# An FFT mixer with two MLPs on Trainium2: two fetches later, five subtractions on another engine, the units at a step's head

## The chip, the cores and the metric

One core of one Trainium2 chip runs the whole program. The metric is the device time of one execution in microseconds (us); of several runs the median is given. TensorE is called PE below, VectorE DVE, ScalarE ACT, GpSimd POOL, SyncE SP; SP issues nearly all transfers, in the order of its queue.

## The reference, cut to what matters

```python
X = np.fft.rfft(x, axis=1)                       # x: 4 x 3136 x 256, float32
y = np.fft.irfft(X * (filt_r + 1j * filt_i), n=3136, axis=1)

u = y + ((y.transpose(0, 2, 1) @ U) @ V).transpose(0, 2, 1)      # U: 3136 x 32
x = u + np.maximum(u @ w_ch1, 0.0) @ w_ch2                       # 256 -> 1024 -> 256

xn = (x - mean(x)) / np.sqrt(var(x) + 1e-06) * g_ln
out = x + np.maximum(xn @ w1b, 0.0) @ w2b
```

U, V and the weights of both MLPs are float64; the kernel works on their bits and cuts them into a high and a low float32r part. Products in the first MLP are made of three matmuls (high by high, high by low, low by high).

## The kernel before, in words

The Fourier transform of length 3136 is done as products with tables, in stages of 56 and 28 points. Batch 0 is transformed first (class First): `rows` makes products of x and tables while x arrives, `columns` runs over 14 columns and for each does a transpose (line 660), the second stage (674), the filter on DVE and POOL (641 to 649: two multiplications by the filter pair f, then a difference and a sum on POOL), and three columns later the third stage (685), whose results DVE adds up (629) and ACT copies out. The tables' last part, uq, is made from u on the way (uf, line 570, then copies on ACT).

Then comes the main loop, a list of steps (phase, f). A phase is a or b (first or second MLP) and a block of 512 tokens; f is one of eight slices of the hidden layer. A step does m1 (line 828: six matmuls, then relu to hh on ACT and the rest hl on DVE) for its own f, and m2 (lines 847 to 849 or 855, 856) for the step two before it. Into this list other work is set by hand:

- a *unit* (function unit) makes 448 tokens of the first MLP's input out of the transformed rows: products psu with the table ic (line 805, or 790 for the first four, the direct units), the low-rank part (810, 792), and the split in high and low (ACT line 223, DVE line 226). It is called by units_to. Each block needs one or two units, and the step sets where: after m2 of the steps with f = 3 and 6 of an a phase, until the next block has its units. A unit takes two of the three PSUM banks of the pool ps_h, which m1 and the second stage use too, in rotation.
- the transforms of batches 1 to 3 (function fft, a generator that advance moves on, at the end of a step, when there is no unit): stage1, then the second stage (stage2, line 345, two banks of ps_h, read by ACT as zc and by DVE as ya) and back (lines 379 and 385).
- the conversions of the weights, `pr` (function stagger), one slot at each next(pr): to32 turns 64-bit numbers into float32 parts by four DVE operations (words, lines 971 to 977) and a POOL product (989); lower (1032, 1034) makes the low part: a difference t - hi on the engine `aside`, then a sum on POOL. The first four slots only fetch (stg); FETCHES says after which transfers of x two and two of them come. EXTRA and SPARE say which of the first steps have a slot more or less.
- todo, a list of small operations for the steps to come (sums, statistics, stores).

`aside` is DVE at first and becomes POOL after `rows`, ahead of `columns` (line 1145 follows `rows`).

Of the kernel before, what the change touches and what calls it, by code (L numbers as in the profile page):

```python
# [34 lines left out]
PUS, UTURN = ((), (0, 1), (2,), (3,), (4,), (5,), (6,)), (0, 1, 2, 3, 4, 6)  # L35
BACKL = 3
AHEAD = 3
FETCHES = (1, 4, 6, 6)

SLOTS, UAHEAD = 4, 2  # L40
PACE = 4
# [11 lines left out]
XLAST = (2, 3), 4, 6, (8, 9), (10, 11, 12)  # L53
SLATE = {**XLATE, 1: 8}
RLATE = {**XLATE, 2: 3}
EXTRA, SPARE = (0, 1, 2, 5, 6), range(13, 20)
BW = 32
LN_EPS = 1e-6

# [128 lines left out]
def fft_mixer_kernel(ctx: ExitStack, tc: tile.TileContext, x, U, V, flt, w1, w2, gln, w1b, w2b,  # L188
# [58 lines left out]
    held = {}  # L247
    NCH = NM // 2
    NGR = NM // 4
    room = [False]  # L250
    todo = []

    def defer(n, act):
# [31 lines left out]
    def fft(b):  # L285
# [138 lines left out]
        for i in range(NGR + 1):  # L424
            yield 2
            if i < NGR:
                stage2(i)
            if i and room[0]:
                back(i - 1, True)
            if 0 < i < NGR and not room[0]:  # L430
                yield 0
            if i and i - 1 in ys:
                back(i - 1, False)
            if i == NGR:
                break
            if i + 1 < NGR:
                loadf(i + 1, 0)
            cross(i)
            yield 0
            if i + 1 < NGR:  # L440
                loadf(i + 1, 1)
            if i + 2 < NGR:
                load2(i + 2)
            yield 0
            total(i)
# [374 lines left out]
    def m1(ph, f):  # L820
        kind, k = ph
        n = blen(k)
        wh, wl = wts["w1" if kind == "a" else "w1b"]
        ah, al = acth[k], actl[k]
        ps = ps_h.tile([P, 512], F32, tag="h", name="psh")
        fs = slice(f * P, (f + 1) * P)
        for j, (w, a, kt) in enumerate([(w, a, kt) for kt in range(KT) for w, a in ((wh, ah), (wh, al), (wl, ah))]):
            nc.tensor.matmul(ps[:, :n], w[:, kt, fs], a[:, kt, :n], start=j == 0, stop=j == 3 * KT - 1)  # L828
        hh = mp.tile([P, BLK], F32R, tag="hh", name="hh", bufs=3)
        hl = mp.tile([P, BLK], F32R, tag="hl", name="hl", bufs=3)  # L830
        nc.scalar.activation(out=hh[:, :n], in_=ps[:, :n], func=AF.Relu)  # L831
        nc.vector.scalar_tensor_tensor(out=hl[:, :n], in0=ps[:, :n], scalar=0.0, in1=f32(hh[:, :n]),  # L832
                                       op0=ALU.max, op1=ALU.subtract)
        hid[ph, f] = hh, hl
# [283 lines left out]
    def load_v():  # L1118
        v_sb = held["v"] = const.tile([P, N], F32R, tag="v", name="v_sb")
        nc.gpsimd.dma_start(v_sb[:3 * R].rearrange("p (h n) -> p h n", h=2), vd.rearrange("h a r n -> (a r) h n"))  # L1120

    with tc.manual_schedule():
        nc.vector.memset(ones, 1.0 / D)
        make_identity(nc, ident)
        warm = ps_t.tile([P, 512], F32, tag="t", name="warm")
        for _ in range(WARM):
            nc.tensor.matmul(warm[:, :P], ones, ones, start=True, stop=True)

        def chain():
            for b in range(1, NB):  # L1130
                yield from fft(b)

        first = First()
        pr = stagger([w_job("w1", w1, 0, "wt"), w_job("w1", w1, 1, "wt"), v_job(0), v_job(1)] + [w_job(nm, w, j) for nm, w, j in (
            ("w2", w2, 0), ("w2", w2, 1), ("w1", w1, 2), ("w1", w1, 3), ("w2", w2, 2),
            ("w2", w2, 3), ("w1b", w1b, 0), ("w1b", w1b, 1), ("w2b", w2b, 0), ("w1b", w1b, 2), ("w1b", w1b, 3),
            ("w2b", w2b, 1), ("w2b", w2b, 2), ("w2b", w2b, 3))])
        first.load(pr)
        for j, _ in enumerate(first.rows()):
            if j < AHEAD:  # L1140
                first.filters(j)
            for _ in range(ROWSLOTS.count(j)):
                next(pr)
        for i in range(KT):
            nc.sync.dma_start(g_sb[i * 64:(i + 1) * 64], gln[:, i].rearrange("(q k) -> q k", k=KT))
        aside = nc.gpsimd
        for j in first.columns():
            for _ in range(COLSLOTS.count(j)):
                next(pr)
            if j == VSTEP:  # L1150
                load_v()
        mixed = first.mixed()
        next(mixed)
        for u in range(2):
            first.part(u, mixed if u == 0 else None)
            next(mixed, None)
        rest = chain()
        state = [0, -9]

        def advance(idx, ph, f):  # L1160
            last = idx - state[1]
            a = ph[0] == "a" and ph[1] >= LEAD
            room[0] = a and f > 2 or ph[0] == "b" and ph[1] >= LEAD - 1 and f < 1
            want = state[0]
            if want == 1 and (last < 2 or idx < FFT1):
                return
            if want == 2 and (last < 3 or f in (2, 5) and ph in ahead and emitted <= need(ahead[ph])):
                return
            if want == 2 and 1 in tstk and not room[0]:
                return  # L1170
            if want:
                state[1] = idx
            state[0] = next(rest, 0)

        def need(k):
            return min((k * BLK + blen(k) - 1) // UN, NUNIT - 1)

        phases = [("a", k) for k in range(LEAD)] + [("b", k) for k in range(LEAD - 1)]
        for k in range(LEAD, NBLK):
            phases += [("a", k), ("b", k - 1)]  # L1180
        phases.append(("b", NBLK - 1))
        ahead = {("a", k): k + 1 for k in range(NBLK - 1)}
        ahead["b", LEAD - 2] = ahead.pop(("a", LEAD - 1))
        loaded, emitted, stored = DIRECT, 0, DIRECT

        def load_to(i):
            nonlocal loaded
            while loaded <= min(i, NUNIT - 1) and loaded // UPB in tstk and (loaded >= UPB or loaded < stored):
                load_unit(loaded)
                loaded += 1  # L1190

        def units_to(i, most=99):
            nonlocal emitted
            while emitted <= i and most > 0:
                assert emitted // UPB in tstk
                load_to(emitted)
                unit(emitted)
                emitted += 1
                load_to(emitted)
                most -= 1  # L1200

        def leftover():
            nonlocal stored
            for u in range(2, UPB):
                first.part(u)
                stored = max(stored, u + 1)
                yield
            wb = const.tile([P, 4, KT * FF], F32R, tag="wb", name="wb")
            wts["w1b"] = [wb[:, j].rearrange("p (a f) -> p a f", a=KT) for j in range(2)]
            pair = wb[:, 2:4].rearrange("p j n -> p (j n)")  # L1210
            held["w2b"] = pair.rearrange("p (f n) -> p f n", f=FT)
            wts["w2b"] = [held["w2b"][:, :, j * D:(j + 1) * D] for j in range(2)]
            nc.gpsimd.dma_start(s2_sb, c_s2)
            nc.gpsimd.dma_start(s3_sb, c_s3)
            yield

        later = leftover()
        units_to(need(0))
        half = FT // 2
        steps = [(ph, h * half + f) for h in range(2) for ph in phases[:2] for f in range(half)]  # L1220
        steps += [(ph, f) for ph in phases[2:] for f in range(FT)]
        for idx in range(len(steps) + 2):
            if idx < len(steps):
                ph, f = steps[idx]
                if ph[0] == "a" and f == 0:
                    units_to(need(ph[1]))
                m1(ph, f)
                load_to(emitted)
                split = f in (3, 6) and ph in ahead and emitted <= need(ahead[ph])
                if not split:  # L1230
                    next(pr, None)
            for act in todo.pop(0) if todo else ():
                act()
            if idx >= 2:
                m2(*steps[idx - 2])
                if steps[idx - 2][1] == FT - 1:
                    end(steps[idx - 2][0])
            if idx < len(steps):
                if split:
                    units_to(need(ahead[ph]), 1)  # L1240
                    next(pr, None)
                elif idx >= FFT0:
                    advance(idx, ph, f)
                if idx in PARTS:
                    next(later, None)
                if idx in UPARTS:
                    first.u_parts(UPARTS.index(idx))
                if idx not in SPARE:
                    next(pr, None)
                if idx in EXTRA:  # L1250
                    next(pr, None)
# [32 lines left out]
```

## Time and profile before

| what | us |
|---|---|
| median of 3 runs | 1321.02 (1318.98 to 1323.53) |
| the profiled execution | 1320.31 |
| its span in the profile | 1318.5 |
| PE, PEld busy | 1303.9, 1042.0 |
| DVE, ACT, POOL busy | 804.5, 425.3, 152.8 |

A span begins with the first instruction of the program and ends with the last; the execution's own time has 1.8 us more around it. Busy time is the union of an engine's instructions. PE's matmuls overlap in the profile, so that its busy share says little; the distance from one matmul's start to the next one's tells how fast it goes. The clock granted to PE was 0.999 of full speed over the span.

### The profile page before, as it was taken

Reading aid. Unit: us, or ns where it says so; the run is one execution under the profiler, and the core shown is the slowest. Engines: PE = TensorE matmul, PEld = TensorE weight load, DVE = VectorE, ACT = ScalarE, POOL = GpSimd, SP = SyncE. Lnnn points to the kernel's source line nnn. Section 1 sums busy time; section 2 is a strip of 40 time slices with the busy share of each in tenths; the row PEclk is TensorE's granted clock in tenths of the full one; section 3 lists DMA queues with packets and bytes.
Section 4 is the critical chain, followed back from the end, with each engine's and each line's share of the span. In section 5 each row is a group of like instructions: output and inputs, shape, how many; then the busy total and the mean of one; then the engine's idle time right before and its main releaser. Section 6 shows DMA issues by size and latency. Waiting matters only on the chain.

```text
span 1318.5 us, 22249 instructions
## 1 busy us (share of the span) xinstructions
PE 1303.9 (99%) x8606; PEld 1042.0 (79%) x8606; DVE 804.5 (61%) x1643; ACT 425.3 (32%) x849; POOL 152.8 (12%) x133
## 2 busy tenths in 40 slices
PE   9999999999999999999999999999999999999998
PEld 8678877777778787787777877878888888888887
DVE  4879976666555557566656565665555545455454
ACT  4655532333222323223232233232222222222222
POOL 0956520211000101000001010000000000000000
PEclk9999999999999999999999999999999999999999
DMA  9655465665572545433456355322202211210121
GB/s 245 177 134 147 116 182 182 200 183 145 147 210 86 144 110 168 135 109 107 141 169 186 88 170 145 104 66 66 56 18 59 66 33 52 66 49 4 45 49 41
DMA packets 167105, 151.58 MB, mean 115 GB/s; under 512 B 66488, under 2 KB 143144, under 8 KB 167000
## 3 DMA queue, kind: packets, MB, share of 16 engines
q1 hardware_dynamic: 166696, 148.70, 39.7%
q0 software_dynamic: 304, 1.47, 0.5%
q8 instruction: 68, 1.11, 0.4%
q14 instruction: 37, 0.30, 0.1%
HBM read 91.10 MB, written 47.54 MB: 105 GB/s over the span
## 4 chain that ended last, share of the span: by engine, by line
PE 92%; DVE 3%; DMA 2%; ACT 1%; issue 1%; SPq 0%; POOL 0%; DVEq 0%; ACTq 0%
PE psh L828 40%; PE pso L855 14%; PE pso L856 7%; PE pso L847 7%; PE pso L848 6%; PE pso L849 6%; PE psu L805 2%; PE ps L305 2%; PE ps L345 1%; PE ps L379 1%; PE psu L810 1%; PE ps L685 1%; PE pt L385 1%; DMA x<-x 1%; DMA stg<-v 1%; PE ps L674 1%
## 5 line engine op out<-in xcount | busy, mean ns | idle before, releaser
L832 DVE SCALAR_TENSOR_TENSOR hl<-psh,hh 128x512 fp32r<-128x512 f32 (+1 forms) x400 | 271.7, 680 | 360.9 <-ACT hh L831 359.2
L831 ACT ACTIVATE hh<-psh 128x512 fp32r<-128x512 f32 (+1 forms) x400 | 235.4, 589 | 676.3 <-PE psh L828 674.1
L855 PE MATMUL pso<-wb,hh 128*128 128x512 f32 x784 | 285.0, 397 | 0.8 <-DVE x L870 0.3
L828 PE MATMUL psh<-ah,wb 128*128 128x512 f32 (+1 forms) x800 | 279.9, 391 | 0.3 <-DVE hl L832 0.3
L856 PE MATMUL pso<-wb,hl 128*128 128x256 f32 x784 | 219.5, 280 | 0.0
L828 PEld LDWEIGHTS psh<-ah,wb 128*128 128x128 f32 x800 | 149.7, 188 | 45.8 <-issue 5.7
L855 PEld LDWEIGHTS pso<-wb,hh 128*128 128x128 f32 x784 | 147.3, 188 | 36.4 <-DVE x L870 1.6
L828 PE MATMUL psh<-ah,w1h 128*128 128x512 f32 (+1 forms) x400 | 157.6, 394 | 1.0 <-DVE hl L832 1.0
L847 PE MATMUL pso<-hh,w2h 128*128 128x512 f32 (+1 forms) x400 | 156.5, 391 | 0.3 <-DVE x2t L896 0.3
L828 PE MATMUL psh<-al,wb 128*128 128x512 f32 (+1 forms) x400 | 155.5, 389 | 0.0
L828 PE MATMUL psh<-al,w1h 128*128 128x512 f32 (+1 forms) x400 | 155.1, 388 | 0.1
L828 PE MATMUL psh<-ah,w1l 128*128 128x512 f32 (+1 forms) x400 | 154.3, 386 | 0.0
L848 PE MATMUL pso<-hl,w2h 128*128 128x512 f32 (+1 forms) x400 | 154.0, 385 | 0.0
L849 PE MATMUL pso<-hh,w2l 128*128 128x512 f32 (+1 forms) x400 | 154.0, 385 | 0.0
L856 PEld LDWEIGHTS pso<-wb,hl 128*128 128x128 f32 x784 | 147.9, 189 | 7.4
L361 POOL TENSOR_TENSOR xs<-xs,ft 128x512 f32<-128x512 f32 x42 | 53.9, 1290 | 642.3 <-DMA xs<-zc 485.5
L828 PEld LDWEIGHTS psh<-ah,w1h 128*128 128x128 f32 x400 | 75.1, 188 | 23.2 <-issue 5.7
L896 DVE SCALAR_TENSOR_TENSOR x2t<-pso,ln,x2t 128x256 f32<-128x256 f32 x196 | 89.7, 480 | 4.3 <-PE pso L856 0.9
L847 PEld LDWEIGHTS pso<-hh,w2h 128*128 128x128 f32 x400 | 75.1, 188 | 20.5 <-issue 5.9
L828 PEld LDWEIGHTS psh<-ah,w1l 128*128 128x128 f32 x400 | 75.2, 188 | 15.9
L849 PEld LDWEIGHTS pso<-hh,w2l 128*128 128x128 f32 x400 | 75.1, 188 | 15.2
L848 PEld LDWEIGHTS pso<-hl,w2h 128*128 128x128 f32 x400 | 75.2, 188 | 14.8 <-issue 0.5
(153 smaller groups left out, 1335.5 us busy)
## 6 DMA issues: line engine op xcount, KB each, us to landing
ft<-flt SPq DMA_DIRECT2D x42, 512.0 KB
xd<-x SPq DMA_DIRECT2D x96, 128.0 KB
x2t<-xd SPq DMA_DIRECT2D x24, 512.0 KB
wt<-bd SPq DMA_DIRECT2D x48, 224.0 KB
out<-x2t SPq DMA_DIRECT2D x84, 128.0 KB
xs<-zc SPq DMA_DIRECT2D x84, 128.0 KB
xt<-x SPq DMA_DIRECT2D x84, 112.0 KB
zd<-ze SPq DMA_DIRECT2D x84, 112.0 KB
```

Of the source, the lines that this page charges most:

```text
L305: nc.tensor.matmul(pss[j][quarter(h), m * D:(m + 1) * D], ct[rows56(j), 2 * h + m], xs[h][rows56(j), m], start=True, stop=True)
L361: nc.gpsimd.tensor_tensor(out=xs, in0=xs, in1=fi[:, e], op=ALU.mult)
L805: nc.tensor.matmul(pss[h][c * HALF:(c + 1) * HALF, dh, h * spare + m:h * spare + half:UW], t[rows, m, d0:d0 + HALF], ic[rows, m, :], start ...
L828: nc.tensor.matmul(ps[:, :n], w[:, kt, fs], a[:, kt, :n], start=j == 0, stop=j == 3 * KT - 1)
L831: nc.scalar.activation(out=hh[:, :n], in_=ps[:, :n], func=AF.Relu)
L832: nc.vector.scalar_tensor_tensor(out=hl[:, :n], in0=ps[:, :n], scalar=0.0, in1=f32(hh[:, :n]), op0=ALU.max, op1=ALU.subtract)
L847: nc.tensor.matmul(o, wh[:, f, ds], hh[:, :n], start=f == 0, stop=False)
L848: nc.tensor.matmul(o, wh[:, f, ds], hl[:, :n], start=False, stop=False)
L849: nc.tensor.matmul(o, wl[:, f, ds], hh[:, :n], start=False, stop=f == FT - 1)
L855: nc.tensor.matmul(o, hh[:, cs], w, start=f == 0, stop=False, skip_group_check=True)
L856: nc.tensor.matmul(o[:, D:], hl[:, cs], w[:, :D], start=False, stop=f == FT - 1, skip_group_check=True)
L896: nc.vector.scalar_tensor_tensor(out=o, in0=acc[c][:, half * D:(half + 1) * D], scalar=rs[:, c:c + 1], in1=o, op0=ALU.mult, op1=ALU.add)
```

## The change

- FETCHES loses its last two entries, and the two slots that fetch the halves of V come in `rows`, behind the filters of the first column.
- `aside` becomes POOL behind `columns` and not ahead of it.
- EXTRA goes from steps 0, 1, 2, 5, 6 to 0, 1, 4, 5, 8.
- A unit is issued ahead of the step's m1 and not behind its m2. Where the step before has run a second stage together with its back (joint), the unit comes right behind them; while the second stage goes on, it is otherwise only issued at f over 5.
- advance is no longer held back at f = 5.

```diff
-FETCHES = (1, 4, 6, 6)
+FETCHES = (1, 4)
...
-EXTRA, SPARE = (0, 1, 2, 5, 6), range(13, 20)
+EXTRA, SPARE = (0, 1, 4, 5, 8), range(13, 20)
...
-    room = [False]
+    room, joint = [False], [False, -9]
...
             if i < NGR:
                 stage2(i)
+            joint[0] = 0 < i < NGR
             if i and room[0]:
                 back(i - 1, True)
+                joint[1] = True
...
             if j < AHEAD:
                 first.filters(j)
+            if j == 0:
+                for _ in range(4 - len(FETCHES)):
+                    next(pr)
...
-        aside = nc.gpsimd
         for j in first.columns():
...
                 load_v()
+        aside = nc.gpsimd
...
-            if want == 2 and (last < 3 or f in (2, 5) and ph in ahead and emitted <= need(ahead[ph])):
+            if want == 2 and (last < 3 or f == 2 and ph in ahead and emitted <= need(ahead[ph])):
                 return
...
             state[0] = next(rest, 0)
+            if joint[1] is True:
+                joint[1] = idx
...
+                split = ph in ahead and emitted <= need(ahead[ph]) and (joint[1] == idx - 1 or f > 5 if joint[0] else f in (3, 6))
+                if split:
+                    units_to(need(ahead[ph]), 1)
                 m1(ph, f)
                 load_to(emitted)
-                split = f in (3, 6) and ph in ahead and emitted <= need(ahead[ph])
-                if not split:
-                    next(pr, None)
+                next(pr, None)
...
-                if split:
-                    units_to(need(ahead[ph]), 1)
-                    next(pr, None)
-                elif idx >= FFT0:
+                if not split and idx >= FFT0:
                     advance(idx, ph, f)
```

Three places of the order show what this moves. The names are those of the program; the changed kernel's lines stand two or so further down.

SP's queue at the end of x's transfers (x), where the tables e and d, the filter pairs f, and the 64-bit halves of V (stg<-v) are fetched. Before:

```order
L473 DMA x_176<-x 112x1024
L965 DMA stg<-v 128x784 x2
L482 DMA e_184<-c_e 112x256
L483 DMA e_184<-c_p 128x256
L486 DMA d_187<-c_d 128x2x112
L487 DMA d_188<-c_d 128x2x112
L598 DMA f_227<-flt 32x2x512 x4
L598 DMA f_301<-flt 32x2x512 x4
```

Changed:

```order
L475 DMA x_176<-x 112x1024
L484 DMA e_180<-c_e 112x256
L485 DMA e_180<-c_p 128x256
L488 DMA d_183<-c_d 128x2x112
L489 DMA d_184<-c_d 128x2x112
L600 DMA f_223<-flt 32x2x512 x4
L967 DMA stg<-v 128x784 x2
L600 DMA f_301<-flt 32x2x512 x4
```

The two fetches of V have moved behind e, d and the first filter pair.

DVE at the first direct unit inside the loop, steps 2 to 4: the subtractions of the unit (al<-psu), those of m1 (hl<-psh), copies of transposes (wt0<-psw) and the conversion (cyh, ct). Before:

```order
L736 COPY wt0_1186<-psw_1187 112x512
L975 SCALAR_TENSOR_TENSOR ct_1155<-cyh_1148,ct_1155 128x512
L977 TENSOR_SCALAR cyh_1148<-ct_1155 128x512
L832 SCALAR_TENSOR_TENSOR hl_1212<-psh_1204,hh_1211 128x512
L226 TENSOR_TENSOR al_1066<-psu_1221,ah_1065 128x128
L226 TENSOR_TENSOR al_1230<-psu_1221,ah_1229 128x320
L226 TENSOR_TENSOR al_1066<-psu_1233,ah_1065 128x128
L226 TENSOR_TENSOR al_1230<-psu_1233,ah_1229 128x320
```

Changed:

```order
L738 COPY wt0_1186<-psw_1187 112x512
L977 SCALAR_TENSOR_TENSOR ct_1155<-cyh_1148,ct_1155 128x512
L226 TENSOR_TENSOR al_1066<-psu_1196,ah_1065 128x128
L226 TENSOR_TENSOR al_1205<-psu_1196,ah_1204 128x320
L226 TENSOR_TENSOR al_1066<-psu_1208,ah_1065 128x128
L226 TENSOR_TENSOR al_1205<-psu_1208,ah_1204 128x320
L834 SCALAR_TENSOR_TENSOR hl_1226<-psh_1218,hh_1225 128x512
L979 TENSOR_SCALAR cyh_1148<-ct_1155 128x512
```

The unit's four subtractions have moved ahead of the m1's hl and of the conversion's last step.

PE at one of the seven units that the change joins to a second stage: second stage (ps<-zt), back (ps<-ya and pt<-ya), unit (psu). Before, from the end of an m2 to the next m1; the second stage comes only after that m1 and another m2:

```order
L847 MATMUL pso<-hh,w2h 128x512
L848 MATMUL pso<-hl,w2h 128x512
L849 MATMUL pso<-hh,w2l 128x512
L805 MATMUL psu<-ic,wt 64x56 x32
L810 MATMUL psu<-v_sb,tk 128x256 x4
L828 MATMUL psh<-ah,w1h 128x512
```

Changed:

```order
L851 MATMUL pso<-hh,w2l 128x512
L345 MATMUL ps_5392<-zt,s_sb 64x512
L345 MATMUL ps_5393<-zt,s_sb 64x512
L379 MATMUL ps_5412<-ya,s_sb 64x256 x4
L379 MATMUL ps_5413<-ya,s_sb 64x256 x4
L385 MATMUL pt<-ya,uh_sb 32x256 x4
L807 MATMUL psu<-ic,wt 64x56 x32
L812 MATMUL psu<-v_sb,tk 128x256 x4
L830 MATMUL psh<-ah,w1h 128x512
```

Second stage and back have moved one step up, and the unit stands right behind them.

## Rows read from the trace of the kernel before

**Rows 1.** The page, busy time and instructions of each engine; GB/s in 40 slices.

```profile
PE 1303.9 (99%) x8606; PEld 1042.0 (79%) x8606; DVE 804.5 (61%) x1643; ACT 425.3 (32%) x849; POOL 152.8 (12%) x133
...
GB/s 245 177 134 147 116 182 182 200 183 145 147 210 86 144 110 168 135 109 107 141 169 186 88 170 145 104 66 66 56 18 59 66 33 52 66 49 4 45 49 41
```

**Rows 2.** Timeline of PE, near 660 us: start, length (us), engine, line, operation.

```profile
662.72 0.39 PE L847 MATMUL pso<-hh,w2h 128*128 128x512 f32 x1
...
664.08 0.39 PE L828 MATMUL psh<-ah,wb 128*128 128x512 f32 x1
```

**Rows 3.** Timeline of PE, 486 to 502 us: unit and second stage in the loop.

```profile
491.14 0.39 PE L847 MATMUL pso<-hh,w2h 128*128 128x512 f32 x1
...
492.60 1.16 PE L805 MATMUL psu<-ic,wt 56*64 56x56 f32 x64
...
494.25 0.40 PE L828 MATMUL psh<-ah,w1h 128*128 128x512 f32 x1
...
495.63 0.39 PE L847 MATMUL pso<-hh,w2h 128*128 128x512 f32 x1
...
497.08 1.09 PE L345 MATMUL ps<-zt,s_sb 56*64 56x512 f32 x8
...
499.59 0.50 PE L828 MATMUL psh<-ah,w1h 128*128 128x512 f32 x1
...
501.08 0.39 PE L847 MATMUL pso<-hh,w2h 128*128 128x512 f32 x1
```

**Rows 4.** The windows, columns stage: PE, PEld, DVE, ACT, POOL busy; clock; DMA share; GB/s.

```profile
40.00:46.60 6.60, 4.95 (x38) 2.93 (x35) 5.21 (x14) 3.20 (x11) 6.60 (x9) 1.00 0.73 191
46.60:52.00 5.40, 5.38 (x54) 3.86 (x54) 5.33 (x10) 3.48 (x10) 5.36 (x6) 1.00 0.35 92
```

**Rows 5.** The chain that ended last, first 60 us: start, us, what.

```profile
17.31 11.34 DMA stg<-v
...
28.67 4.58 DMA f<-flt
```

**Rows 6.** Timeline of all engines, 26 to 48 us; in brackets idle before and what ended it.

```profile
30.77 1.08 PE L674 MATMUL ps<-z,e 112*64 112x256 f32 x8 [0.25 <-ACT z L223]
...
33.43 0.69 DVE L641 TENSOR_TENSOR hl<-ps,f 128x512 f32<-128x512 f32 x1 [2.71 <-PE psz L660]
...
34.63 0.68 DVE L570 TENSOR_SCALAR uf<-pst,w_sb 128x448 f32<-128x448 f32 x1
...
37.37 1.42 PE L685 MATMUL ps<-d,hl 64*128 64x144 f32 x16 [1.43 <-ACT d L223]
...
41.06 0.53 PE L685 MATMUL ps<-d,ya 64*128 64x144 f32 x4 [0.67 <-POOL ya L648]
...
43.16 1.26 POOL L1032 TENSOR_TENSOR ct<-ct,w1h 128x512 f32<-128x512 f32 x1
...
46.62 1.22 PE L685 MATMUL ps<-d,hl 64*128 64x144 f32 x14 [0.71 <-DVE d L629]
```

**Rows 7.** Timeline, 100 to 115 us: DVE line 975 with POOL at work, and without.

```profile
106.01 1.59 POOL L1034 TENSOR_TENSOR w2l<-ct,cyl 128x512 fp32r<-128x512 f32 x1
...
106.25 1.90 DVE L975 SCALAR_TENSOR_TENSOR ct<-cyh,ct 128x512 int32<-128x512 int32 x1
...
114.23 0.68 DVE L975 SCALAR_TENSOR_TENSOR ct<-cyh,ct 128x512 int32<-128x512 int32 x1
```

**Rows 8.** Timeline, 80 to 104 us: the first direct unit inside the loop.

```profile
91.56 0.68 DVE L832 SCALAR_TENSOR_TENSOR hl<-psh,hh 128x512 fp32r<-128x512 f32 x1
...
93.57 1.04 PE L790 MATMUL psu<-ic,wt 112*128 112x112 f32 x8
...
96.92 0.47 PE L828 MATMUL psh<-ah,w1h 128*128 128x512 f32 x1 [0.98 <-DVE hl L832]
...
98.79 0.40 PE L847 MATMUL pso<-hh,w2h 128*128 128x512 f32 x1
```

**Rows 9.** Timeline, 486 to 502 us: DVE reads the second stage.

```profile
498.99 1.29 DVE L352 TENSOR_TENSOR ya<-ps,ft 128x512 f32<-128x512 f32 x2 [0.20 <-ACT zc L351]
```

## The prediction

> **What bounds the kernel now.** I read the page first: TensorE (PE) is busy 99% of the span [rows 1]. A busy PE is not yet PE at its pace, so the second view is the timeline of PE alone, step by step, where the start of each group shows how long the one before really took. In the main loop a step is six products of m1 and six or eight of m2. An m2 of the a kind that leads to another m1 takes 1.36 us (662.72 to 664.08) [rows 2]. Around a unit and a second stage the same lengths return each time [rows 3]: the m2 ahead of a unit takes 1.46 us (491.14 to 492.60), the unit 1.65, the m1 behind it 1.38, the m2 ahead of a second stage 1.45, second stage with back 2.51 (497.08 to 499.59), and the m1 behind that 1.49. So in the loop PE goes from one product to the next, and what can be won there is the price of changing over: about 0.10 us into a unit (1.46 less 1.36) and 0.11 us out of a back (1.49 less 1.38).
>
> PE waits for others mainly in the columns stage, from 34 to 47 us, and around the first unit inside the loop, near 94 us. From 40.0 to 46.6 us POOL is busy 6.60 of 6.60 us and PE only 4.95; from 46.6 to 52.0 PE is full again (5.38 of 5.40), with VectorE (DVE) at 5.33 and POOL at 5.36 beside it [rows 4]. The reader should see that the change touches a place where three engines are nearly full, and that PE alone is worth time.
>
> **The fetches.** Two transfers stg<-v of 392 KB leave the SP queue ahead of e, d and the first filter pair f and go behind that pair. In the chain of waits stg<-v ends the wait at 28.65, f is issued at 28.67 and takes 4.58 us more, to 33.25 [rows 5]; only then does DVE multiply, at 33.43, after 2.71 us idle [rows 6]. At the 245 GB/s of the first slice [rows 1], 784 KB are 3.2 us, so f should be there near 30.1. Next late is then PE: the products that the multiplication reads start at 30.77 [rows 6] and end near 31.8. So the multiplication starts near 31.9 instead of 33.43: 1.5 us earlier. The way from uf (34.63) to the first product of the third stage (37.37) is ACT and POOL work of 2.74 us and shifts along; PE waited 1.43 us there [rows 6]. What speaks a little against it: ACT's conversion of v stands in ACT's queue between the copies of z, and v lands later than now. I take 1.4 us off at 37.37.
>
> **The differences.** Five subtractions (line 1032: one for each of two w1 quarters, two v halves, one w2 quarter) leave POOL for DVE. One costs POOL 1.26 us (43.16) [rows 6]; that one stands right ahead of a wait, and PE's waits for POOL and DVE at 41.06 and 46.62 are 0.67 and 0.71 us [rows 6]. On DVE no such subtraction is in the trace in this stage; the nearest row is the conversion's own step with two inputs in SBUF, 128x512, at 0.68 us while POOL is idle and 1.90 us while POOL works (106.25, beside POOL's 106.01) [rows 7]. These are the two ends. I take 0.68, because every subtraction that moves also removes 1.26 us of POOL work that could stand in the way. The first falls into DVE's 2.71 us idle, the second into DVE's wait for the last products of u; the other three lie where DVE has only 0.07 us in 5.40 left [rows 4], but there PE reads DVE's results three columns later, so they are covered as long as DVE doesn't fall a column (about 2.8 us) behind. If that cover is gone, 3 x 0.68 = 2.0 us come back. Fetches and differences together: I take 1.6 us off by the time of the product at 46.62, with 4.0 us off (every wait of the stretch) and 1.0 us added as the ends.
>
> A rule of the Trainium skill speaks against this edit. SBUF — State Buffer, section Who interferes with whom: a DVE instruction with two inputs in SBUF contends with a GpSimd instruction that reads SBUF, and the later one waits until the other is through. The trace agrees (0.68 against 1.90). By that rule alone all five would cost 1.90, or 9.5 us of DVE time; that is a rival below.
>
> **Units at the head.** All 26 units of the loop (2 direct, 24 of the other kind) are issued one step earlier. For 17 of the 24 the neighbours on PE are the same kinds (m2 before, m1 behind), the banks rotate in the same order and nothing is gained or lost. Their loads move ahead of two output stores in SP's queue, which nobody waits for.
>
> The first direct unit gains. Now it starts at 93.57, the m1 behind it at 96.92 after 0.98 us of waiting for DVE's hl, and that m1 takes 1.87 us (to 98.79) where 1.38 is usual, for it reads what the unit just made [rows 3, 8]: 1.47 us in all. Changed, another m1 and m2 stand between the unit and its reader, and DVE has the unit's subtractions ahead of the conversion's last step. In exchange the unit, at about 93.57 - 2.8 = 90.8, needs for its second half (1.1 us in, 91.9) the bank that hl frees at 91.56 + 0.68 = 92.24 [rows 8]: 0.4 us of new wait. Net 1.1 us off, ends 1.5 off and nothing. The second direct unit has no wait now and may get the same new one: 0.2 us added, ends 0 and 0.4.
>
> **Joined units.** Seven units now stand right behind second stage and back, where one m1 and m2 stood between. Each saves the 0.10 into the unit and the 0.11 out of back, and pays the change from back to unit, which the trace doesn't show: between 0 and the 0.11 of the exit, I take 0.10. The bank that the unit's second half takes is the second stage's first. Its last reader is DVE's ya, two from 498.99, 1.29 us together: the first is through at about 499.63, 2.55 us after the stage's start at 497.08, and the unit would start 2.51 us after it [rows 3, 9]. With the signal that is a wait of 0.1 us, 0.2 where DVE is late. Net about 0; for seven, 0.1 us off, with 1.5 us off (7 x 0.21) and 1.4 added (7 x 0.2) as ends. A rule that touches this: TensorEngine Tiling (Array Packing), Key Properties, says that changing the tiling mode drains TensorE, so by it the join saves one drain of five each time; taken at the 0.10 of the rows this is again 0.7 us for seven, without the wait for the bank.
>
> One unit follows a joined one after two steps instead of three: its load has 1.65 + 2 x 2.8 = 7.2 us. A load as slow as the 4.58 us of f [rows 5] fits; if SP issues it late, up to 1 us is added. Taken as 0.
>
> **Conversion slots.** Extra slots move from steps 2 and 6 to 4 and 8: same count, so nothing; the cover is that PE waits nowhere for a converted weight. If it is gone, one slot is half a step, 1.4 us.
>
> **The sum.** -1.6 -1.1 +0.2 -0.1 = -2.6 us. The profiled execution took 1320.31 us (span 1318.5), so 1317.7; the median of the runs is 0.7 above the profiled one, so 1318.4.
>
> **Rivals.**
> *More waits go than I count* (chance 0.30). POOL is full from 40.0 to 46.6 [rows 4] and loses 1.26 us there: the waits 1.43, 0.67 and 0.71 all go (2.8), the direct unit keeps its whole 1.5, the joins their 1.5: 5.8 off, 1315.2. Against it: the new waits on banks are real order.
>
> *The joined unit waits for the second stage's banks* (0.07), the case of the other side. If DVE is behind when ya is due, each joined unit stands like the direct unit now, 0.98 us [rows 8]: 7 x 0.98 = 6.9, so 1325.3, slower. It decides from about 0.95 us a join. Against it: DVE was idle 0.20 us before ya, waiting for ACT [rows 9].
>
> *DVE becomes the bound of the columns stage* (0.08). By the rule on the shared port the three late differences cost 1.90 each, PE follows DVE, the 1.6 is lost and some 2.7 more: 1322.7. For it: 5.33 of 5.40 [rows 4]. Against it: POOL has less work to collide with.
>
> *The fetches change nothing* (0.05): f is slow by itself, at 4.58 us for 128 KB issued last [rows 5], and the start stays: 1320.0.
>
> **The numbers.** A measurement of this kernel can tell about 0.3%, 4.0 us, from no change: faster is below 1317.1, slower above 1325.0. My forecast has 0.50, with 0.05 of it below 1317.1; its own range is 1316.5 to 1320.5. Faster 0.30 + 0.05 = 0.35; the same 0.45 + 0.08 + 0.05 = 0.58; slower 0.07. The range 1314.5 to 1322.7 leaves out the slower case, some 0.07 of the faster one and some 0.04 of the DVE case.
>
> **What would show it.** First multiplication near 31.9, the third stage's first product near 36.0, the product of 46.62 near 45; no 0.98 us wait for hl at the direct unit, a 0.4 us one inside it; the m1 behind a joined unit at 1.38, and the group second stage, back, unit at 4.2 to 4.4 us. It is wrong if the multiplication still starts after 33, if DVE is without a gap from 46 to 70 with PE waiting for hl or ya, or if a joined group takes over 5 us.

## The result and the profile after

The changed kernel took 1328.31 us (median of 7 runs, 1322.29 to 1331.23) against 1320.96 for the kernel before (7 runs, 1318.98 to 1323.53): a ratio of 1.0055, 95% interval 1.0041 to 1.0068, so 7.3 us slower. The forecast was 1318.4 with a range up to 1322.7. The sign was wrong, and the range did not hold the time. Six of the seven runs took 1326.6 us or more, at a mean granted clock of 0.996 to 0.998; the seventh kept 1.000 and took 1322.29.

The page of the changed kernel, with the rows that answer to [rows 1]:

```profile
span 1329.5 us, 22251 instructions
...
PE 1308.5 (98%) x8606; PEld 1046.4 (79%) x8606; DVE 807.4 (61%) x1648; ACT 425.4 (32%) x849; POOL 147.8 (11%) x128
...
PEclk9999999999999999999999999999999999999999
```

PE has the same 8606 instructions, is busy 4.6 us longer (1308.5 for 1303.9) and idle for some 6 us more. The page hides the cause, for its slices are 33 us wide and its digits coarse. The view by windows shows it. The columns are the window, its length, the busy time (and count) of PE, PEld, DVE, ACT and POOL, the granted clock of PE, the DMA share and GB/s:

```profile
42.00:46.00 4.00, 2.72 (x25) 1.79 (x22) 4.00 (x8) 1.77 (x6) 3.85 (x5) 0.99 0.74 199
46.00:50.00 4.00, 4.00 (x18) 2.08 (x18) 2.96 (x8) 1.77 (x5) 2.92 (x4) 0.58 0.79 209
111.00:114.00 3.00, 1.43 (x12) 1.14 (x11) 3.00 (x5) 0.88 (x2) 1.43 (x2) 1.00 1.00 264
114.00:117.00 3.00, 3.00 (x11) 2.39 (x10) 1.68 (x5) 0.99 (x3) 2.92 (x3) 0.54 0.80 194
202.00:206.00 4.00, 2.25 (x68) 1.57 (x68) 2.37 (x4) 0.08 (x1) 0.00 (x0) 1.00 0.85 299
206.00:210.00 4.00, 4.00 (x27) 3.31 (x17) 1.48 (x4) 1.44 (x5) 0.00 (x0) 0.57 0.53 171
```

They stand in pairs. Three times PE is idle for a third to a half of a window, and in the next one its clock is near 0.5, the 1.2 GHz level. In the kernel before the clock was 1.00 in all of these stages. Its windows around the second and third pair, 4 us or so earlier:

```profile
107.00:110.00 3.00, 3.00 (x18) 2.52 (x17) 3.00 (x5) 2.03 (x4) 1.43 (x2) 1.00 0.40 105
110.00:113.00 3.00, 3.00 (x23) 2.83 (x22) 2.52 (x5) 0.94 (x3) 2.92 (x3) 1.00 1.02 319
198.00:202.00 4.00, 4.00 (x81) 3.41 (x80) 2.51 (x5) 0.98 (x2) 0.00 (x0) 1.00 0.62 206
202.00:206.00 4.00, 4.00 (x31) 2.85 (x30) 2.90 (x9) 2.03 (x5) 0.00 (x0) 1.00 0.63 198
```

The waits of PE name the places:

```profile
PE pz L539 <- DVE u L515: 2.9, 1, 2.9
PE pz L539 <- DMA x<-x: 2.3, 4, 1.4
PE psu L807 <- DVE ze L311: 1.7, 1, 1.7
PE psu L792 <- DVE hl L834: 1.6, 1, 1.6
PE psu L807 <- DMA wt<-bd: 1.3, 2, 1.0
```

(The columns are us in total, times, longest; lines of the changed kernel stand 2 to 5 lines further down.) Three of the five rows are units: psu at line 792 is a direct unit, at 807 one of the other kind. None of these three is in the kernel before.

To see what each is worth I laid the starts of all 400 m1 groups of both traces side by side, counting steps from 0. The changed kernel is 4.0 us behind at the first m1, and gets 3.4 further behind over step 7 (the second direct unit), 3.6 over step 35 (the first unit of the other kind), and 1.6 over step 206. Around the first direct unit it wins 1.2, at the joins some 0.1 each, and everywhere else it keeps its distance. So in this execution, the slowest of the seven, four places hold the whole loss.

### The profile page after: what moved, and what is told of

The parts are those of the page before. It is cut to its first block, busy times and chain, and to the rows that moved or that the text cites. A ratio compares the mean times of both kernels' runs of the same rounds, so it can differ in the third digit from the quotient of the medians.

```text
span 1329.5 us, 22251 instructions
## 1 busy us (share of the span) xinstructions
PE 1308.5 (98%) x8606; PEld 1046.4 (79%) x8606; DVE 807.4 (61%) x1648; ACT 425.4 (32%) x849; POOL 147.8 (11%) x128
## 4 chain that ended last, share of the span: by engine, by line
PE 87%; DVE 5%; DMA 4%; ACT 1%; SPq 1%; issue 1%; POOL 0%; DVEq 0%; ACTq 0%
PE psh L830 39%; PE pso L857 13%; PE pso L858 7%; PE pso L849 6%; PE pso L850 6%; PE pso L851 6%; PE psu L807 2%; PE ps L345 1%; PE ps L379 1%; PE ps L305 1%; PE psu L812 1%; DMA f<-flt 1%; DVE hl L834 1%; DMA x<-x 1%; DMA e<-c_e 1%; PE pt L385 1%
```

## The experiments

The first question is which part of the change loses. Each was made alone.

**e1, the start alone**

```diff
-FETCHES = (1, 4, 6, 6)
+FETCHES = (1, 4)
...
+            if j == 0:
+                for _ in range(4 - len(FETCHES)):
+                    next(pr)
...
-EXTRA, SPARE = (0, 1, 2, 5, 6), range(13, 20)
+EXTRA, SPARE = (0, 1, 4, 5, 8), range(13, 20)
-        aside = nc.gpsimd
         for j in first.columns():
...
+        aside = nc.gpsimd
```

> Only the start of the change: the two fetches of v moved from the row stage's slots to two steps at its first slot, the five differences given back to VectorE, the new extra slots; units and joins as before. Theory (the loss is made of separate places, and the start is one of them): the first m1 starts about 4.0 us later than before (82.17 to 86.2), with TensorE at 1.2 GHz for some us behind the wait for the first multiplies, time about 1325. Rival A (my forecast for this part): -1.6 us, about 1319.4. Rival B (the late start of the profiled run was only that execution's transfers, which were behind already at 12.8 us where the program is still the same): within 1 us of before, 1320 to 1322.

Measured: 1320.81 against 1320.41, ratio 1.0006 (0.9997 to 1.0015). First m1 at 81.46. The late start of the changed kernel's profile was that execution's own: its row stage ended at 32.6 us, while the row stages of all other executions of this study, changed start or not, ended between 27.5 and 29.8.

**e2, the units alone** (head of the step, joins, advance; the start as before)

```diff
+                if split:
+                    units_to(need(ahead[ph]), 1)
                 m1(ph, f)
...
-                if split:
-                    units_to(need(ahead[ph]), 1)
-                    next(pr, None)
```

> Only the units: all of the units at a step's head, the joins and the advance of the transform; the start as before. Theory: from the profiled pair -1.2 (first unit of the direct kind), +3.4 (the second, which waits for VectorE and is then run at 1.2 GHz), +3.6 (the first loaded unit, the same with VectorE's ze and the load), +1.6 (the unit at step 206, a load), -0.5 (joins): +6.9, about 1328. Rival A (the units are late only because the start is): about 1320, with no stretch at 1.2 GHz behind a unit. Rival B (the forecast for these parts): 1320.

Measured: 1327.98, ratio 1.0060 (1.0047 to 1.0074). The units are the loss. Step by step: +0.2 over the first direct unit, +0.9 over the second, +5.6 over step 35, -0.45 for the joins, +1.4 over step 206.

**e3, the joins alone** (units without a second stage in their period stay behind m2)

```diff
+                head = split and joint[0]
+                if head:
+                    units_to(need(ahead[ph]), 1)
                 m1(ph, f)
...
+                if split and not head:
```

> Only the joins: units of a period that has both go to the head behind the second stage, all others stay behind the second layer as before; the start as before. Theory: joins -0.5, the unit behind a joined one (step 206) up to +1.6, no stretch at 1.2 GHz: 1320.5 to 1322. Rival (moving behind the second stage itself makes PE wait for banks, 0.7 a join): about 1326.

Measured: 1324.23, ratio 1.0026 (1.0017 to 1.0035): more than the theory had. In the trace everything happens in one place. The timeline of e3, step 205 to 207:

```profile
759.13 0.86 SPq L762 DMA_DIRECT2D wt<-bd  x2
...
763.90 0.32 PE L807 MATMUL psu<-ic,wt 56*64 56x56 f32 x4 [1.44 <-DMA wt<-bd]
764.53 1.14 PE L807 MATMUL psu<-ic,wt 56*64 56x56 f32 x60 [0.31 <-DMA wt<-bd]
...
766.19 0.63 PE L830 MATMUL psh<-ah,w1h 128*128 128x512 f32 x1
766.61 0.63 PE L830 MATMUL psh<-al,w1h 128*128 128x512 f32 x1
...
769.84 0.39 PE L849 MATMUL pso<-hh,w2h 128*128 128x512 f32 x1
770.06 0.39 PE L850 MATMUL pso<-hl,w2h 128*128 128x512 f32 x1
```

The unit of step 206 stands two steps behind a joined one. Its load is issued only behind that unit, at 759.13, and PE waits 1.44 and 0.31 us for it. Behind the wait the matmuls follow each other every 0.42 us, from 769.6 on every 0.22 again. The step costs 3.6 us: some 1.7 of waiting, the rest at 1.2 GHz (half speed, which the trace has for 3.4 us). In e2 the same wait was 1.1 us in all, the clock stayed, and the step cost 1.4.

**e4, the fetches alone** (the FETCHES lines of e1)

> Only the fetches of v moved, nothing else. Theory (what makes the start late is that v now stands in the queue beside the filters and its words come late to VectorE): first m1 3 to 4 us later than before, about 1324.5. Rival A (the forecast: the filter pair lands earlier, first multiply 1.5 us earlier): about 1319.5. Rival B (the start's loss belongs to the differences or slots or to that execution): within 1 us of before.

Measured: 1319.81, ratio 0.9997 (0.9988 to 1.0005). Its timeline:

```profile
31.91 0.69 DVE L641 TENSOR_TENSOR hl<-ps,f 128x512 f32<-128x512 f32 x1 [1.18 <-PE ps L674]
```

This is the row that stood at 33.43 [rows 6]. DVE now waits for PE and not for the filter, and the time, 31.91, is the forecast's 31.9. The row stage ended at the same time in both executions (28.89 and 28.88), so the two times can be compared. From the end of the row stage's last product to the first m1 it takes 51.8 us here and in e12, and 52.3 to 53.5 in the eight executions with the old start: about 1.1 won. The timed ratio alone does not show it: -0.4 us, between -1.6 and 0.7. With the differences too (e1, e10, e11) it is 53.3 again. Rows of e1, its timeline:

```profile
38.63 0.69 DVE L1032 TENSOR_TENSOR ct<-ct,w1h 128x512 f32<-128x512 f32 x1
...
45.12 1.22 PE L685 MATMUL ps<-d,hl 64*128 64x144 f32 x14 [1.13 <-DVE d L629]
...
46.50 1.10 DVE L1032 TENSOR_TENSOR ct<-ct,vh 128x392 f32<-128x392 f32 x1
...
69.47 1.50 POOL L1034 TENSOR_TENSOR w2l<-ct,cyl 128x512 fp32r<-128x512 f32 x1
70.93 0.73 POOL L648 TENSOR_TENSOR hl<-hl,hh 128x256 f32<-128x256 f32 x1
...
71.72 0.52 PE L685 MATMUL ps<-d,hl 64*128 64x144 f32 x4 [0.90 <-POOL hl L648]
```

The five differences cost DVE 0.65, 0.69, 1.10, 1.08 and 0.68 us. PE waits for DVE's d 1.13 where it waited 0.71 [rows 6], and 0.90 at 71.72 for POOL, whose sum ahead of that product (70.93) starts 42.8 us behind the end of the row stage, as in the kernel before. What the fetches win, the differences give back.

The next four runs take the late units apart. First the one of step 206, in three ways that differ from e3 by one thing each.

**e5, the unit of step 206 back behind m2**

```diff
-                head = split and joint[0]
+                head = split and joint[1] == idx - 1
```

> e3 with one thing undone: the unit of step 206, two steps behind a joined one, goes back behind the second layer, one m1 and one m2 (2.76 us) later. Theory (all of e3's +3.8 us is this one unit's wait for its load, 1.4 and 0.3 us, and the matmuls at 1.2 GHz behind it): about 1320.3, no stretch at 1.2 GHz between 760 and 780 us, joins -0.4 over steps 60 to 205. Rival A (the joins themselves cost): about 1324. Rival B (the unit waits there too, since its load is still issued only behind the joined unit): 1322 to 1324.

Measured: 1320.34 against 1319.79, ratio 1.0001 (0.9992 to 1.0010). The loss is gone. In the trace the seven joins win 0.05 to 0.14 us each, 0.57 together, too little for the timed ratio to show.

**e6, its load issued earlier**

```diff
                 emitted += 1
-                load_to(emitted)
+                load_to(emitted + (emitted == 16))
```

> e3 with TensorE's order untouched and only the load of the unit of step 206 (three transfers) issued one unit earlier, at step 187 instead of behind the joined unit of step 204. Theory (the wait is the load's and the 1.2 GHz stretch follows the wait): both go, about 1320.3. Rival (the place on TensorE is what costs: banks, or an m1 whose inputs are late): 1322 to 1324 as e3.

Measured: 1319.50, ratio 1.0001 (0.9992 to 1.0009). PE's order is e3's to the last instruction, and the loss is gone, so the place on PE was not at fault. The unit in the timeline of e6:

```profile
760.23 1.15 PE L807 MATMUL psu<-ic,wt 56*64 56x56 f32 x64
761.31 0.74 PE L812 MATMUL psu<-v_sb,tk 96*128 96x256 f32 x4
```

**e7, matmuls in the wait** (`fill` writes so many products of m1's shape, which nobody reads, into the next bank of ps_h, so that from there on the rotation is one bank further)

```diff
+                if idx == 206:
+                    fill(ph, f, 7)
                 if head:
                     units_to(need(ahead[ph]), 1)
```

> e3 with seven matmuls put ahead of the unit of step 206, whose result nobody reads (7 x 0.23 = 1.6 us, as long as the wait); the unit waits for the same load until the same time. Theory (the wait and the clock are two costs: about 1.7 and 2.1 us of the +3.6): the clock stays at 2.4 GHz, the six m1 matmuls behind the unit come every 0.23 us instead of 0.43, and the time falls by about 2 to 1322.2. Rival (the slow matmuls belong to the load's traffic or to the unit, not to TensorE's idle time): no stretch goes, 1324 or 1 to 2 us more for the added matmuls.

Measured: 1321.66, ratio 1.0014 (1.0006 to 1.0023). Each against the kernel before as timed beside it, e3 lost 3.4 us and e7 loses 1.9: some 1.6 us less, although PE does more work. In the traces step 206 costs 3.6 and 1.65 us. Timeline of e7:

```profile
761.92 1.75 PE L1226 MATMUL fill<-ah,w1h 128*128 128x512 f32 x7
763.60 1.36 PE L807 MATMUL psu<-ic,wt 56*64 56x56 f32 x64
...
765.46 0.40 PE L830 MATMUL psh<-ah,w1h 128*128 128x512 f32 x1
765.69 0.40 PE L830 MATMUL psh<-al,w1h 128*128 128x512 f32 x1
```

The windows of e3 and of e7, the same stretch:

```profile
760.00:764.00 4.00, 2.56 (x14) 1.82 (x13) 2.45 (x9) 0.60 (x1) 1.38 (x2) 1.00 0.95 309
764.00:769.00 5.00, 4.69 (x75) 3.95 (x75) 1.47 (x4) 1.32 (x4) 0.00 (x0) 0.72 1.01 298
```

```profile
760.00:764.00 4.00, 4.00 (x34) 3.10 (x35) 2.10 (x7) 0.60 (x1) 0.67 (x1) 1.00 0.97 290
764.00:769.00 5.00, 5.00 (x80) 4.34 (x76) 2.17 (x6) 1.81 (x5) 0.00 (x0) 1.00 0.99 278
```

The unit starts as late as in e3, DMA is as busy (1.01 and 0.99), and the clock stays at 1.00. So the slow matmuls follow PE's idle time, not the load's traffic. The wait and the clock are two costs of about the same size.

**e8, the same at step 35, in e2**

```diff
+                if idx == 35:
+                    fill(ph, f, 11)
                 if split:
```

> e2 with eleven matmuls whose result nobody reads (2.5 us) ahead of the unit of step 35, which there waits 2.5 us for VectorE's ze and then runs at 1.2 GHz. Theory: the unit ends no earlier than ze lets it, but the 1.2 GHz stretch of 201 to 206.5 us goes, worth 2 to 2.7 us, about 1325.5. Rival (not the clock but ze's place is the whole cost, or the slow stretch comes from something else): 1328, or up to 2.5 more where the added matmuls push the unit.

Measured: 1325.82, ratio 1.0048 (1.0035 to 1.0061). Each against the kernel before as timed beside it, the loss is 6.3 us where e2's was 7.9, some 1.6 less; the theory had 2 to 2.7. In the trace step 35 costs 2.7 us here and 5.6 in e2, and the clock is 1.00 in the windows around it. The 2.7 left are the eleven matmuls (2.72 us), which stand for the wait.

**e9, one unit alone at its head**

```diff
+                head = split and idx == 35
+                if head:
+                    units_to(need(ahead[ph]), 1)
                 m1(ph, f)
```

> The kernel before with one unit alone moved: that of step 35, the first loaded one, to its step's head, 13 matmuls earlier on TensorE. Theory (in e2 the m1 starts went from +1.27 to +6.83 us over this one step: 2.5 us of wait for VectorE's ze, the rest the matmuls at 1.2 GHz behind it): +5 to +5.6, about 1325. Rival (in e2 it was late because the units ahead of it had been moved too, and VectorE was behind): less than +1, 1320 to 1321.

Measured: 1322.87 against 1319.84, ratio 1.0024 (1.0012 to 1.0035); less than the theory's +5, because two costs come and go apart. Of the nine runs the five with a mean granted clock of 0.999 or 1.000 took 1321.0 to 1322.9, the four with 0.997 or 0.998 took 1324.0 to 1325.6. The means of the two groups lie 3.3 us apart. The profiled one is of the second kind:

```profile
195.99 0.32 PE L805 MATMUL psu<-ic,wt 56*64 56x56 f32 x4
...
197.13 1.29 DVE L311 TENSOR_TENSOR ze<-ps,zb 128x512 f32<-128x512 f32 x2 [1.79 <-DMA zd<-ze]
...
198.47 1.96 PE L805 MATMUL psu<-ic,wt 56*64 56x56 f32 x60 [2.15 <-DVE ze L311]
```

```profile
200.00:205.00 5.00, 5.00 (x28) 4.14 (x22) 1.61 (x5) 1.91 (x5) 0.00 (x0) 0.50 0.52 163
```

Four products of the unit go into its first bank, then PE waits 2.15 us for DVE to read ze out of the second, where the first stage of the transform had put it a step earlier. DVE itself waits for the store zd to free ze's old place. Behind that the clock is at 0.50 for the five microseconds shown, 6.8 us in all; at half speed that is 3.4 us of lost work, as far as the two groups of runs lie apart. In the kernel before the same rows read:

```profile
197.73 1.29 DVE L311 TENSOR_TENSOR ze<-ps,zb 128x512 f32<-128x512 f32 x2 [1.51 <-DMA zd<-ze]
...
199.66 1.16 PE L805 MATMUL psu<-ic,wt 56*64 56x56 f32 x64
```

There ze was out at 199.02, and the unit came 0.64 us later. Started at its step's head, 196.79, it had to stand 1.9 us or so. That could be read before the change was run.

Last, the change with its late units put back.

**e10, two units back** (steps 35 and 206; **e11** adds step 7 to the list)

```diff
+                head = split and idx not in (35, 206)
+                if head:
+                    units_to(need(ahead[ph]), 1)
                 m1(ph, f)
...
+                if split and not head:
+                    units_to(need(ahead[ph]), 1)
```

> The whole change, with two units put back behind the second layer: those of steps 35 and 206. The two units of the direct kind stay at their steps' heads. Theory: what is left are the direct units, +0.2 and +0.9 in e2, -1.2 and +3.4 in the changed kernel's profile: 1321.5 to 1323. Rival (only the two waits counted): as e11, 1320.5.

Measured: 1321.51, ratio 1.0012 (1.0003 to 1.0020). PE waits 1.6 us inside the second direct unit for hl, and that step costs 3.4 us in the trace, the same as in the changed kernel, whose rows are:

```profile
110.25 1.04 PE L792 MATMUL psu<-ic,wt 112*128 112x112 f32 x8
110.31 1.56 POOL L1036 TENSOR_TENSOR w2l<-ct,cyl 128x512 fp32r<-128x512 f32 x1
110.55 1.88 DVE L977 SCALAR_TENSOR_TENSOR ct<-cyh,ct 128x512 int32<-128x512 int32 x1
...
112.35 0.68 DVE L834 SCALAR_TENSOR_TENSOR hl<-psh,hh 128x512 fp32r<-128x512 f32 x1
...
113.09 1.15 PE L792 MATMUL psu<-ic,wt 112*128 112x112 f32 x8 [1.57 <-DVE hl L834]
```

The hl that frees the bank stands in DVE's queue behind a conversion step of 1.88 us. This is the slow row of [rows 7], 1.90 us beside POOL's work, now in PE's way.

**e11, three units back**

> The whole change, with three units put back behind the second layer: those of steps 7, 35 and 206; the other 21 at the head or behind the second stage. Theory (these three are the whole loss): the start's +0.4 of e1 less the joins' 0.4 and what the first direct unit gives (-1.2 to +0.2): 1319 to 1320.5, no stretch at 1.2 GHz behind a unit. Rival (the other moved units cost too, or the parts of the change work against each other): 1322 or more.

Measured: 1319.19, ratio 0.9997 (0.9989 to 1.0006). With 3 of its 26 moved units put back the change loses nothing. Nothing is won either, though.

**e12, the candidate** (e6 with the fetches of e4)

> The candidate: e6 (joins, the load of step 206 issued one unit earlier, all other units as before) with the two fetches of v moved as in e4. Theory: the gains add where they were seen in the traces, -0.9 left of the fetches and -0.5 of the joins: 1318.5 to 1319.3, the first verdict below the kernel before if any. Rival (what the start gains is given back at the loads and VectorE's queue, and what the joins gain is below what can be measured): 1319.5 to 1320.5.

Measured: 1318.34 against 1319.84, ratio 0.9991 (0.9982 to 0.9999). It is the only kernel of the study whose interval lies below 1, by 1.2 us (0.1 to 2.4), and only just. Its parts are the fetches and the joins with their load in time; neither is clear of no change by itself (e4, e6), so how the 1.2 us divide between them is not shown.

## Why the prediction was wrong

*The failed step* is the sentence "For 17 of the 24 the neighbours on PE are the same kinds, the banks rotate in the same order and nothing is gained or lost." It was read off one unit of the loop near 492 us [rows 3] and held for 15 of the 17. One of the other two is step 206, whose load the prediction treated apart (below). The other, at step 35, is the first unit of its kind and stands right behind a first stage of the transform, so its second bank is one that DVE has still to empty. e9 shows it alone: 3.2 us slower (1.6 to 4.6); in its trace the wait is 2.15 us, with the clock behind it.

*The load of the unit behind a joined one* ("up to 1 us is added. Taken as 0"): the mechanism was right, the size wrong. In e3 the load took 4.8 us from its issue at 759.13, near the 4.58 used as a bound, but SP issued it 2.3 us after the joined unit's end (756.83). The wait is 1.1 to 1.75 us, and 3.6 with the clock (e3). e6 shows that it is the load alone.

*The second direct unit* ("0.2 us added, ends 0 and 0.4"): the wait for hl came, as 0.66 us in e2's trace and 1.57 in the changed kernel's. The bound was taken from the first direct unit, where hl was late by 0.4; here it stands behind a 1.88 us step. e10 less e11 gives 2.3 us for it, where the step itself costs 3.4 in e10's trace: what e11 saves there it loses again in part, 1.15 at step 26, where PE then waits for hl.

*What no step had* is the clock. Each wait was priced at its length. e7 and e8 show that a wait here can cost about twice that: with the clock kept, each loses some 1.6 us less by the timed ratios, 1.9 and 2.8 by the traces. The changed kernel's one run at a clock of 1.000 took 1322.29, 4.3 us less than the next. The Trainium skill, TensorE: Matmul & The Clock Gate, section HAM oscillation — how this bites in real kernels, describes matmuls that run at half rate behind a wait for a transfer; the traces agree, 0.42 us from matmul to matmul where 0.22 is usual, though the waits in its example are longer than those here. With it the rivals on the slow side would have been dearer and likelier.

*The fetches and differences* (-1.6): first multiplication at 31.91 in e4, forecast 31.9; the third stage's first product at 36.92 in e4 and 35.14 in e1, forecast 36.0; the product of 46.62 at 45.12 in e1, forecast near 45. The last of these is luck in part: e1's row stage ended 0.7 us earlier than that of the kernel before, and counted from there the product comes 0.8 earlier, not 1.6. The fetches' part is right, about 1.1 at the first m1 by the traces. The differences' 0.68 each was right for three and 1.10 for the two of 392 columns, but their cover was thinner than argued: what they added came back as PE's waits of 1.13 and 0.90 us. The timed ratio of e1, 1.0006, holds no gain. The rival "DVE becomes the bound" (2.7 slower at the worst) pointed the right way and was too dear.

*The first direct unit* (-1.1): 1.2 less in the changed kernel, but for another reason. e1, which does not move this unit, wins 1.4 there, and e2, which moves it under the old start, wins nothing: PE then waits 1.03 us for al instead of 0.98 for hl. The number came out, by luck. What takes the wait away is, by the order on DVE, the extra slot moved from step 2: in e1 the conversion's last step (DVE line 977) stands behind hl and the unit's subtractions, where in the kernel before it stands ahead of both, at 94.80 for 1.37 us. e2 has the old slots and the old order (94.94, 1.40 us), and e4, which leaves EXTRA as it was, wins nothing there. So the extra slots, for which the prediction took nothing, decide at this unit. Timeline of e1:

```profile
93.98 0.68 DVE L832 SCALAR_TENSOR_TENSOR hl<-psh,hh 128x512 fp32r<-128x512 f32 x1
...
96.96 0.42 DVE L977 TENSOR_SCALAR cyh<-ct 128x512 int32<-128x512 int32 x1
...
165.69 0.50 PE L828 MATMUL psh<-ah,wb 128*128 128x512 f32 x1 [1.42 <-DVE hl L832]
```

The last row is step 26, where e1 gives 1.15 of it back: PE waits 1.42 us for hl, 0.3 in the kernel before.

*The joins* (-0.1 for seven): the right sign, and 0.57 in e5's trace, inside the ends given. There a joined group takes 4.30 us, the forecast said 4.2 to 4.4, and no bank is waited for. Timeline of e5:

```profile
492.90 1.09 PE L345 MATMUL ps<-zt,s_sb 56*64 56x512 f32 x8
...
494.81 1.29 DVE L352 TENSOR_TENSOR ya<-ps,ft 128x512 f32<-128x512 f32 x2 [1.84 <-ACT zc L351]
...
495.40 1.29 PE L807 MATMUL psu<-ic,wt 56*64 56x56 f32 x64
...
497.20 0.40 PE L830 MATMUL psh<-ah,w1h 128*128 128x512 f32 x1
```

The 0.7 us by the drain of the Trainium skill, TensorEngine Tiling (Array Packing), Key Properties, came nearer to that than my own sum; no run shows the drain apart from the rest of a join. The rival of the other side had the mechanism that decided, a unit that waits for its second bank, but put it at the joins, where it does not happen.

The sum by places then is 2.3 for step 7, 3.2 for step 35, 1.5 for step 206 without the clock and 3.6 with it, 0.8 (-0.4 to 2.0) for the start, less 0.6 for the joins: 7.2 to 9.3 against the measured 7.3 (5.4 to 9.0).

## What to carry to other kernels

An operation moved forward in an in-order queue loses its slack against everything that it reads or overwrites: its bank's last reader, its load, and the queue that the reader stands in. A periodic schedule can be argued from one period, but its first instance and each irregular spacing need their own rows: look up when the bank was emptied and when the load was issued there. Where TensorE is 99% busy, a wait of one or two microseconds is not worth its length but can cost 2 to 2.5 times that (3.6 us for 1.75 in e3, 5.5 for 2.15 in e9), and work that nobody needs can be cheaper than the wait.

## What the runs showed of the hardware

That the clock falls behind one wait of 1.4 to 2.5 us inside an otherwise full stretch was not expected: after waits of 1.44 and 0.31 (e3), 1.57 (the changed kernel, step 7), 1.67 (the changed kernel, step 35), 2.15 (e9) and 2.53 us (e2) the granted clock was at the 1.2 GHz level for 3.4 us (e3, the changed kernel) or 6.8 us (e2, e9). After 0.8 and 0.3 us (e2, step 206) and 0.66 us (e2, step 7) it did not fall, and neither did it after 1.42 us (e1 and e11, step 26). The same wait of e9 lowered the mean clock in four of nine runs and not in five; what decides that in a run is open, since only one of the nine left a trace. Seven (e7) or eleven (e8) matmuls put into the wait kept the clock.
